# Cluster products of q and k in one TensorE visit, and a unit's filler work from its first gap

## The chip, the cores and the metric

The kernel runs on one core of a Trainium2 chip. The metric is the device time of one execution in microseconds. The median of four runs of the kernel before is 346.37 us (346.23 to 346.71).

A core has five engines that work side by side, each through its own queue in order: TensorE (PE; its weight loads are shown as PEld), VectorE (DVE), ScalarE (ACT), GpSimd (POOL) and SyncE (SP, which only issues transfers here). TensorE writes its results to PSUM, a small memory of eight banks, from which VectorE and ScalarE read them. "Granted clock" is the share of its full speed that TensorE was allowed.

## The reference

Two steps are computed, one feeding the other.

```python
# q, k, v: (4, 8, 768, 64); centroids: (8, 16, 64)
q_assign = argmax(q_n @ c_n.T); k_assign = argmax(k_n @ c_n.T)     # nearest of 16 clusters
scores = where(q_assign[:, None] == k_assign[None, :], q @ k.T / 8, -1e9)
attn = softmax(scores) @ v                                          # 32 heads
# x: (3072, 512), the heads side by side
xn = x / sqrt(mean(x * x) + 1e-6) * rms_g
out = (silu(xn @ w_gate) * (xn @ w_val)) @ w_out                    # 512 -> 1536 -> 512
```

Attention runs only between a query and the keys of the same cluster. The kernel gets the mask from the product itself: to the 64 rows of a head it adds 16 rows of zeros and ones that name the cluster, so a query and a key of the same cluster score a large constant more, and the exponential takes that constant off again.

## The kernel before

**Units and groups.** There are 8 units: for each of the 4 batches, two blocks of 384 queries, with all 8 heads (`UNITS`). A group is 4 heads of one batch (`HG`, 8 groups), and holds the transposed and extended q and k of these heads. Batch b uses groups 2b and 2b + 1.

**One unit.** `attention` walks through the 8 heads with 3 score steps each, so a unit has 24 of them. A score step (`scores`, L333) is two matmuls, and ScalarE turns the result into exponentials (L337). Scores have two PSUM buffers (`ps_s`), so the step after the next needs the exponential of this one to be done. At the second score step of a head, `pv` of the head before is issued (18 short matmuls, L351); after every second head VectorE divides by the sums (L356, L358). In the last head, each of the three steps adds a square on ScalarE (L376; VectorE in the first two units).

**Gaps and filler.** Behind each score step lies a gap, numbered 0 to 23 here, which `attention` fills from a list of pieces, each with a cost. It issues pieces until their summed cost reaches the share of the total that belongs to the gaps passed so far. With `skip=1` the first gap stays empty, and the total is spread over 23. Filler comes in this order:
- the last 8 pieces of the gate and value products of unit u - 2 (`gv`, L423),
- the row norm of unit u - 1 (`rms`),
- the output product of unit u - 2 (`out_mm`, L448) in pieces, with the transposes of the normed rows of unit u - 1 (`xtrans`, L396) among the last of them,
- the other `gv` pieces of unit u - 1 but its last 8, interleaved evenly by `spread` with the preparation of group u + 2 (in units 2 to 5: groups 4 to 7).

A gate piece is four matmuls; ScalarE then computes a tanh (L431) and VectorE a product (L432). A value piece is four matmuls and a product on VectorE (L436).

**Preparing a group** (`group_work`, from unit 2 on by `group`). For each of the 4 heads, `trans` transposes q and k with three f32 matmuls each (L208), and ScalarE copies the result out (L214); GpSimd casts q, and VectorE casts k in two halves (L227); then v is cast and later heads' loads are issued. After the four heads come the clusters, first of q (m = 0) and then of k (m = 1), each in four steps (`cluster_steps`): `products` (four f32 matmuls of 32 columns, L241, and a transpose by VectorE, L244), `most` (L249), `same` (L253) and `back` (L271, another transpose). `products` has cost 0.7, the other three cost nothing, so they follow at once. At the end `place` writes the zeros and ones under q and k with small transfers on GpSimd's queue (L282).

**PSUM banks.** `trans`, `cluster_products`, `xtrans`, `gv` and `out_mm` all take their PSUM tiles from one pool of three banks (`ps_g`). A tile can be written when the last reader of the tile that held its bank has finished. TensorE's queue is in order: where the first matmul of a piece waits for a bank, everything behind it waits too.

The order is the program's own (`manual_schedule`); nothing reorders it later.

Of the kernel before, what the change touches and what calls it, by code (L numbers as in the profile page):

```python
# [22 lines left out]
def kernel(  # L23
# [13 lines left out]
    B, H, S, D = q.shape  # L37
# [8 lines left out]
    NG = B * H // HG  # L46
    UNITS = [(b, c, HT) for b in range(B) for c in (0, HT)]
    NU = len(UNITS)
    CC = DM // P
# [4 lines left out]
    CUT = CC + 2 * FC - 8  # L54
# [30 lines left out]
    def load_qk(n):  # L85
        if n < B * H:
            load(n, 0)
            load(n, 1)

    def load_v(n, vq=None):  # L90
        if n >= B * H:
            return
        stagedv[n] = stage.tile([P, ST, D], F32, tag="vs", name="vs", bufs=NV)
        (vq or nc.sync).dma_start(out=stagedv[n], in_=src(v, n))
# [107 lines left out]
    def trans(g, h, part, on=None):  # L202
        if (g, h // 2) not in qkT:
            qkT[g, h // 2] = qk32.tile([P, 2, 2, UQ], F32, tag="qkT", name="qkT")
        qk = staged[g * HG + h]
        ps = ps_g.tile([P, UQ], F32, tag="gen", name="tq")
        for i in range(HT):
            nc.tensor.transpose(ps[:, i * P:(i + 1) * P], qk[:, part, 2 * i:2 * i + 2].rearrange("p t d -> p (t d)"),  # L208
                                ident_f)
        to, by = qkT[g, h // 2][:, h % 2, part], 1.0 / ZS if part else 1.0  # L210
        if on is nc.vector:
            nc.vector.tensor_scalar_mul(to, ps, by)
        else:
            nc.scalar.activation(to, ps, ACT.Copy, scale=by)  # L214
# [5 lines left out]
    def cast(on, g, h, part, es=(0, 1)):  # L220
        for e in es:
            to = cols((kext if part else qext)[g % 4][:D, h], g, e)
            of = qkT[g, h // 2][e * D:(e + 1) * D, h % 2, part]
            if on is nc.scalar:
                nc.scalar.copy(to, of)
            else:
                on.tensor_copy(to, of)  # L227

    def vcast(n):
        nc.gpsimd.tensor_copy(vbf[n // HG % 4][:, n % HG, :, :D], stagedv[n])  # L230
# [24 lines left out]
    def cluster_steps(g, m):  # L255

        of = {}

        def products():
            of["cl"] = cluster_products(g, [(h, m) for h in range(HG)])  # L260

        def most():
            of["mx"] = largest(of["cl"])

        def same():
            of["ohT"] = asg.tile([P, UQ], BF16, tag="ohT", name="ohT", bufs=2)
            compare(of["ohT"].rearrange("p (b e c) -> p b e c", e=2, c=NC), of["cl"], of["mx"])

        def back():
            put[g, m] = asg.tile([P, UQ], BF16, tag="oh", name="oh", bufs=3)  # L270
            nc.vector.transpose(put[g, m], of["ohT"])  # L271

        return [products, most, same, back]
# [3 lines left out]
    def place(on, g, m, es=(0, 1)):  # L277

        ext = (kext if m else qext)[g % 4]
        for h in range(HG):  # L280
            for e in es:
                on.dma_start(out=ext[D:D + NC, h, e * UQ:(e + 1) * UQ],  # L282
                             in_=put[g, m][32 * h + e * NC:32 * h + (e + 1) * NC])
# [39 lines left out]
    def scores(u, h, i):  # L323
        b, col, nt = UNITS[u]
        g, hh, w = b * 2 + h // HG, h % HG, nt * P
        if i == 0:
            pT[u, h] = ptp.tile([P, ST, UQ], BF16, tag="pT", name="pT")
        n = ST // nt
        ps = ps_s.tile([P, 2, 512], F32, tag="s", name="s")
        flat = ps.rearrange("p a b -> p (a b)")  # L330
        for j in range(n):
            kc = n * i + j
            nc.tensor.matmul(ps[:, j, :w] if nt == HT else flat[:, j * w:(j + 1) * w],  # L333
                             lhsT=cols(kext[g % 4][:KR, hh], g, kc // HT, kc % HT * P, (kc % HT + 1) * P),
                             rhs=cols(qext[g % 4][:KR, hh], g, col // HT, 0, w), start=True, stop=True)
        of = ps[:, :, :w] if nt == HT else flat[:, :n * w].rearrange("p (c w) -> p c w", w=w)
        nc.scalar.activation(pT[u, h][:, n * i:n * i + n, :w], of, ACT.Exp, bias=off, scale=scale * ZS)  # L337
# [130 lines left out]
    def group_work(g):  # L468

        t, c = [], []  # L470
        for h in range(HG):
            n = g * HG + h
            t += [(0.3, lambda h=h: trans(g, h, 0)), (0.3, lambda h=h: trans(g, h, 1))]

            def others(n=n):
                vcast(n)
                load_qk(n + NQ)
                load_v(n + NV)

            def both(h=h, f=others):  # L480
                cast(nc.gpsimd, g, h, 0)
                f()
                cast(nc.vector, g, h, 1, (0,))
            if g == 2:
                c.append((0.0, others))
            else:
                c += [(0.0, both), (0.0, lambda h=h: cast(nc.vector, g, h, 1, (1,)))]
        a = []
        for m in range(2):
            a += [(0.0 if i else 0.7, f) for i, f in enumerate(cluster_steps(g, m))]  # L490
            if g == 3:
                a.append((0.0, lambda m=m: place(nc.gpsimd, g, m)))
            elif g == 2:
                a.append((0.0, (lambda: (place(nc.sync, g, 1), place(nc.sync, g, 0, (1,)))) if m else
                          (lambda: place(nc.sync, g, 0, (0,)))))
        if g > 3:
            a.append((0.0, lambda: [place(nc.gpsimd, g, m) for m in range(2)]))
        return t, c, a

# [4 lines left out]
    def group(g):  # L504
        t, c, a = group_work(g)
        return [x for h in range(HG) for x in t[2 * h:2 * h + 2] + c[2 * h:2 * h + 2]] + a

    def spread(a, b):

        if not a:  # L510
            return list(b)
        w, n = [], 0
        for i, x in enumerate(a):
            w.append(x)
            while n < len(b) * (i + 1) // len(a):
                w.append(b[n])
                n += 1
        return w
# [9 lines left out]
    def out_work(u):  # L528
        return [(0.86, lambda t=t, p=p: out_mm(u, t, p)) for t in range(UNITS[u][2]) for p in range(3)]
# [105 lines left out]
    def attention(heads, fill, skip=0, hooks={}):  # L635
        gaps = [(u, h, i) for u, h in heads for i in range(UNITS[u][2])]
        total, done, n = sum(c for c, _ in fill), 0.0, 0
        for at, (u, h, i) in enumerate(gaps):
            scores(u, h, i)
            if i == (0 if (u, h) == (1, 0) else 1):  # L640
                for p in due:
                    pv(*p)
                due[:] = [(u, h)]
            if h == H - 1:
                squares(u, i, False)
            if (u, h, i) in hooks:
                hooks[u, h, i]()
            while n < len(fill) and at >= skip and done <= total * (at + 1 - skip) / (len(gaps) - skip):
                done += fill[n][0]
                fill[n][1]()  # L650
                n += 1
        for _, f in fill[n:]:
            f()

    attention([(0, h) for h in range(H)], [], hooks={(0, *divmod(i, HT)): f for i in range(H * HT) for f in [first.get(i, more)] if f})
    for u in range(1, NU):
        ffn, o, g = ffn_work(u - 1), out_work(u - 2) if u > 1 else [], u + 2
        if u == 1:
            t, c, a = group_work(2)
            t3, c3, a3 = group_work(3)  # L660
            n = LEAD - 4
            o3 = [(0.0, lambda i=i: load_o(i)) for i in range(0, FC, 4)]
            prep = c + a + spread(weave(t3[n:], c3), o3) + a3[:5]
            idle = const.tile([P, 1], BF16)

            def norm():
                rms(0)
                nc.gpsimd.tensor_copy(idle, xn[0][:, HT - 1, DM - 1:])
                for h in range(HG):
                    casts(pool_, H + h, K0, Q0, K1, Q1)  # L670

            hooks = {(1, 0, 0): late[6], (1, 0, 1): lambda: (late[7](), norm())}
            hooks.update({(1, *divmod(2 + i, HT)): t3[i][1] for i in range(n)})
            hooks[1, *divmod(LEAD - 1, HT)] = lambda: xtrans_all(0)
            fill = spread(ffn[CC:CUT], prep)
            attention([(1, h) for h in range(H)], fill, LEAD, hooks)
        else:
            fill = ffn_work(u - 2)[CUT:] + [(0.0, lambda u=u: rms(u - 1))]
            fill += border(spread(o[:3], [(0.0, f) for _, f in a3[5:]]) + o[3:], ffn) if u == 2 else border(o, ffn)
            attention([(u, h) for h in range(H)], fill + spread(ffn[CC:CUT], group(g) if g < NG else []), 1)  # L680
    rest = ffn_work(NU - 2)[CUT:]
    rest[0][1]()
    pv(NU - 1, H - 1)
# [38 lines left out]
```

The softmax here doesn't subtract the row's maximum and nothing guards it: scores larger than these inputs give would overflow.

## Time and profile before

| | |
|---|---|
| median of the runs | 346.37 us |
| profiled execution | 346.35 us |
| its span, from the first to the last instruction | 344.6 us |
| TensorE busy | 337.7 us, 98% |
| ScalarE busy | 259.6 us, 75% |
| VectorE busy | 220.8 us, 64% |
| GpSimd busy | 113.1 us, 33% |
| granted clock of TensorE | 1.000 |
| score matmuls (L333) | 384, 327 ns each |
| exponentials (L337) | 192, 905 ns each |
| cluster products (L241) | 96 records, 498 ns each |

In the lines of a timeline, the columns are start and duration in us, the engine, the line of the kernel, the operation, the tiles written and read with their shapes, and the number of instructions merged into the row; brackets give how long the engine stood idle before, and what ended that. Matmuls are pipelined: one starts before the one before it has ended. So what a visit of TensorE costs is the time from its start to the start of the next, and not the duration shown. The same holds, by about a tenth of a microsecond, for ScalarE and VectorE. The chain is the work that ended last, followed back from the last instruction.

Each f32 product of a group's clusters shows as two records (two passes), so a visit of four products is eight.

### The profile page before, as it was taken

The page shows a single profiled execution, that of the slowest core. Times are in us where ns is not written, and L with a number is a line of the kernel's source. Part 1 is how long each engine was busy: PE and PEld are TensorE (multiplying, and loading weights), DVE is VectorE, ACT ScalarE, POOL GpSimd, SP SyncE. Part 2 cuts the span into 40 slices and gives each one's busy share as a digit, 9 for nine tenths or more (in the row PEclk, how much of TensorE's full clock was granted, in tenths as well). Part 3 has the DMA queues.
Part 4 walks back from the last instruction along what each step waited for, and adds up shares of the span by engine and source line. Part 5 has one row for each costly group of instructions (what it writes and reads, how often), then busy time and mean ns, then how long its engine had stood idle before and what let it go on. Part 6 is the DMA issues. An engine that isn't in the chain of part 4 may idle for free.

```text
span 344.6 us, 7999 instructions
## 1 busy us (share of the span) xinstructions
PE 337.7 (98%) x3045; PEld 208.6 (61%) x3045; DVE 220.8 (64%) x540; ACT 259.6 (75%) x449; POOL 113.1 (33%) x225
## 2 busy tenths in 40 slices
PE   8999999999999999999999999999999999999996
PEld 4547657555765567565675656755566656655654
DVE  6999796975578626785367745686356645675330
ACT  5899979856888768886797777888778877764422
POOL 6999596234336205180132702435000000000000
DMA  7999989882450014400120010000100001001002
GB/s 269 380 210 205 259 169 232 142 280 82 147 159 17 28 63 150 139 22 35 61 94 2 23 63 31 2 8 18 63 32 0 2 33 61 2 1 64 30 2 91
DMA packets 27302, 31.62 MB, mean 92 GB/s; under 512 B 4480, under 2 KB 24320, under 8 KB 27264
## 3 DMA queue, kind: packets, MB, share of 16 engines
q1 hardware_dynamic: 18608, 25.02, 21.9%
q0 software_dynamic: 8368, 5.71, 10.1%
q8 instruction: 24, 0.39, 0.5%
q10 hardware_dynamic: 288, 0.39, 0.3%
q14 instruction: 14, 0.11, 0.1%
HBM read 28.35 MB, written 6.29 MB: 101 GB/s over the span
## 4 chain that ended last, share of the span: by engine, by line
PE 88%; ACT 5%; DVE 5%; issue 1%; POOL 0%; ACTq 0%; DVEq 0%; POOLq 0%
PE gate L423 17%; PE val L423 17%; PE o L448 17%; PE s L333 16%; PE acc L351 9%; PE tq L208 4%; ACT pT L337 4%; PE sc L241 3%; PE tx L396 1%; PE warm L117 1%; DVE pads L312 1%; DVE kext L317 1%; DVE qext L317 1%; PE o L459 1%; DVE scT L308 1%
## 5 line engine op out<-in xcount | busy, mean ns | idle before, releaser
L337 ACT ACTIVATE pT<-s,off 128x768 bf16<-128x768 f32 x192 | 170.8, 905 | 33.9 <-PE s L333 32.8
L333 PE MATMUL s<-qext,kext 80*128 80x384 bf16 x384 | 94.4, 327 | 1.8 <-ACT pT L337 1.1
L432 DVE SCALAR_TENSOR_TENSOR th<-th,gate 128x384 f32<-128x384 f32 x84 | 46.3, 552 | 51.8 <-ACT th L431 51.5
L423 PE MATMUL gate<-xnT,wg 128*128 128x384 bf16 x384 | 78.6, 325 | 0.1
L423 PE MATMUL val<-xnT,wv 128*128 128x384 bf16 x384 | 78.1, 326 | 0.0
L448 PE MATMUL o<-wo,gvT 128*128 128x512 bf16 x276 | 67.6, 379 | 0.0
L227 POOL CAST qext<-qkT 64x384 bf16<-64x384 f32 x64 | 35.3, 558 | 75.3 <-ACT qkT L214 66.7
L333 PEld LDWEIGHTS <-kext 80*128 80x128 bf16 x384 | 36.6, 98 | 31.4 <-issue 6.4
L431 ACT ACTIVATE th<-gate 128x384 f32<-128x384 f32 x84 | 41.2, 491 | 13.9 <-PE gate L423 13.5
L423 PEld LDWEIGHTS <-wv 128*128 128x128 bf16 x384 | 36.1, 97 | 25.5 <-issue 3.8
L423 PEld LDWEIGHTS <-wg 128*128 128x128 bf16 x384 | 35.9, 97 | 24.5 <-issue 3.3
L436 DVE SCALAR_TENSOR_TENSOR gvT<-th,val 128x384 bf16<-128x384 f32 x84 | 46.2, 550 | 6.2 <-PE val L423 1.6
L351 PEld LDWEIGHTS <-pT 128*128 128x128 bf16 x1152 | 43.4, 97 | 10.1 <-DVE x L358 1.1
L351 PE MATMUL acc<-vbf,pT 128*128 128x65 bf16 x1152 | 45.7, 193 | 0.6 <-ACT pT L337 0.2
L448 PEld LDWEIGHTS <-gvT 128*128 128x128 bf16 x276 | 25.7, 97 | 25.5 <-issue 0.6
L208 PE MATMUL tq<-ident_f,qk 128*128 128x128 f32 x192 | 30.8, 279 | 0.0
L214 ACT ACTIVATE qkT<-tq 128x384 f32<-128x384 f32 x57 | 26.9, 495 | 3.8 <-PE tq L208 3.3
L282 POOL DMA_DIRECT2D qext<-oh x40 | 19.2, 488 | 30.6 <-DVE oh L271 24.2
L397 DVE TENSOR_SCALAR xnT<-tx,gcol 128x384 bf16<-128x384 bf16 x28 | 10.6, 412 | 28.7 <-PE tx L396 28.7
L208 PEld LDWEIGHTS tq<-ident_f,qk 128*128 128x128 f32 x192 | 23.9, 144 | 6.6 <-ACT qkT L214 1.0
L451 ACT COPY o_sb<-o 128x512 f32<-128x512 f32 x23 | 13.5, 586 | 17.7 <-PE o L448 17.7
L282 POOL DMA_DIRECT2D kext<-oh x40 | 19.1, 487 | 9.6 <-DVE oh L271 9.6
(81 smaller groups left out, 247.7 us busy)
## 6 DMA issues: line engine op xcount, KB each, us to landing
qk<-in_q_dram SPq DMA_DIRECT2D x32, 192.0 KB, 3.9
vs<-in_v_dram SPq DMA_DIRECT2D x32, 192.0 KB, 4.2
out_dram<-o_sb SPq DMA_DIRECT2D x23, 256.0 KB, 2.0
qk<-in_k_dram SPq DMA_DIRECT2D x30, 192.0 KB, 4.1
wg<-in_moe_w_gate_dram POOLq DMA_DIRECT2D x4, 384.0 KB, 8.3
wv<-in_moe_w_val_dram POOLq DMA_DIRECT2D x4, 384.0 KB, 10.5
wo<-in_moe_w_out_dram POOLq DMA_DIRECT2D x3, 512.0 KB, 7.6
qext<-oh POOLq DMA_DIRECT2D x40, 12.0 KB, 1.6
```

The lines of the kernel that those rows point to most:

```text
L208: nc.tensor.transpose(ps[:, i * P:(i + 1) * P], qk[:, part, 2 * i:2 * i + 2].rearrange("p t d -> p (t d)"), ident_f)
L214: nc.scalar.activation(to, ps, ACT.Copy, scale=by)
L227: on.tensor_copy(to, of)
L282: on.dma_start(out=ext[D:D + NC, h, e * UQ:(e + 1) * UQ], in_=put[g, m][32 * h + e * NC:32 * h + (e + 1) * NC])
L333: nc.tensor.matmul(ps[:, j, :w] if nt == HT else flat[:, j * w:(j + 1) * w], lhsT=cols(kext[g % 4][:KR, hh], g, kc // HT, kc % HT * P, (kc ...
L337: nc.scalar.activation(pT[u, h][:, n * i:n * i + n, :w], of, ACT.Exp, bias=off, scale=scale * ZS)
L351: nc.tensor.matmul(acc[:, h % 2, t], lhsT=pT[u, h][:, kc, t * P:(t + 1) * P], rhs=vbf[g % 4][:, hh, kc % HT * 2 + kc // HT], start=kc == 0 ...
L423: nc.tensor.matmul(ps, lhsT=w[:, c, f * P:(f + 1) * P], rhs=xnT[u][:, c, :n], start=c == 0, stop=c == CC - 1)
L431: nc.scalar.activation(th, ps, ACT.Tanh, scale=0.5)
L432: nc.vector.scalar_tensor_tensor(th, th, 1.0, ps, op0=ALU.add, op1=ALU.mult)
L436: nc.vector.scalar_tensor_tensor(gvT[u][:, f, :n], gates[u], 0.5, ps, op0=ALU.mult, op1=ALU.mult)
L448: nc.tensor.matmul(outs[u], lhsT=gvT[u][:, f, t * P:(t + 1) * P], rhs=wo[:, f], start=f == 0, stop=f == FC - 1)
```

## The change

Two edits.

```diff
         if g > 3:
+            a[:1] = [(1.4, lambda f=(a[0][1], a.pop(4)[1]): [x() for x in f])]
             a.append((0.0, lambda: [place(nc.gpsimd, g, m) for m in range(2)]))
```

For groups 4 to 7 the list `a` had nine pieces: products, most, same, back of q, the same of k, and place. The fifth, k's products, is taken out and put into one piece with q's, with the summed cost 1.4. The order becomes: products of q and of k (eight f32 products one after the other, and two transposes of L244 on VectorE), most, same, back of q, most, same, back of k, place. As the list is one piece shorter, `spread` also sets all the pieces of the preparation a little differently among the `gv` pieces.

```diff
-            attention([(u, h) for h in range(H)], fill + spread(ffn[CC:CUT], group(g) if g < NG else []), 1)
+            attention([(u, h) for h in range(H)], fill + spread(ffn[CC:CUT], group(g) if g < NG else []))
```

In units 2 to 7 the filler begins in gap 0 and not in gap 1, and its cost is spread over 24 gaps and not 23. The first pieces, of the `gv` of unit u - 2, now stand before the `pv` of the last head of unit u - 1, which is still issued in gap 1.

No matmul, copy or transfer is added or taken away.

## The prediction

> **What bounds the kernel now.** I read the page first (busy time and chain), then the timeline of TensorE gap by gap, and last the VectorE and ScalarE timelines around the places where TensorE stands still.
>
> ```profile
> span 344.6 us, 7999 instructions
> PE 337.7 (98%) x3045; PEld 208.6 (61%) x3045; DVE 220.8 (64%) x540; ACT 259.6 (75%) x449; POOL 113.1 (33%) x225
> PE 88%; ACT 5%; DVE 5%; issue 1%; POOL 0%; ACTq 0%; DVEq 0%; POOLq 0%
> ```
>
> TensorE is the bound: it is never long idle and the chain is its own work. No matmul is added or taken away, so the time can change only through the small delays between visits. I write S, PV, G, V, O, T, C, X for a visit to scores, pv, gate, val, out_mm, trans, cluster_products, xtrans. From start to next start, undisturbed, they take 0.328, 0.547, 0.650, 0.650, 0.864, 0.328, 0.785 and 0.164 us. Whatever a visit takes over that is a delay. From unit 2 on the delays sit in few places, and units 3 to 5 repeat with a period of 41.04 us (C at 100.73, 141.77, 182.81, 223.85 in the chain).
>
> ```profile
> 94.12 0.52 PE L208 MATMUL tq<-ident_f,qk 128*128 128x128 f32 x3
> 94.48 0.81 PE L423 MATMUL gate<-xnT,wg 128*128 128x384 bf16 x4
> ...
> 100.25 0.49 PE L333 MATMUL s<-qext,kext 80*128 80x384 bf16 x2
> 100.67 0.85 PE L241 MATMUL sc<-qkT,cblk 128*32 128x384 f32 x8
> ...
> 106.16 0.49 PE L333 MATMUL s<-qext,kext 80*128 80x384 bf16 x2
> 106.64 0.81 PE L423 MATMUL val<-xnT,wv 128*128 128x384 bf16 x4
> 107.29 0.88 PE L333 MATMUL s<-qext,kext 80*128 80x384 bf16 x4
> ...
> 266.77 0.49 PE L333 MATMUL s<-qext,kext 80*128 80x384 bf16 x2
> 267.53 0.48 PE L333 MATMUL s<-qext,kext 80*128 80x384 bf16 x2 [0.27 <-ACT pT L337]
> ```
>
> Read the starts; the durations overlap and are not what a visit costs. S at 100.25 should hand over at 100.58, C starts at 100.67: 0.09 lost on entering a C visit. S at 106.16 should hand over at 106.49, V comes at 106.64: 0.16 lost, because its PSUM bank is freed by VectorE's L436 of 106.08. The two adjacent S visits at 107.29 take 0.72 in the chain instead of 0.656: 0.07 lost waiting for an exponential. At 266.77 the same meeting of two S costs 0.43 (0.76 to the next start).
>
> ```profile
> 90.62 0.56 DVE L432 SCALAR_TENSOR_TENSOR th<-th,gate 128x384 f32<-128x384 f32 x1 [0.27 <-ACT th L431]
> 91.21 0.36 DVE L227 CAST kext<-qkT 64x384 bf16<-64x384 f32 x1
> 91.60 0.56 DVE L436 SCALAR_TENSOR_TENSOR gvT<-th,val 128x384 bf16<-128x384 f32 x1
> ...
> 104.51 0.55 DVE L432 SCALAR_TENSOR_TENSOR th<-th,gate 128x384 f32<-128x384 f32 x1 [1.06 <-ACT th L431]
> 104.98 0.55 DVE L253 TENSOR_TENSOR ohT<-scT,mx 128x384 bf16<-128x384 f32 x1
> ...
> 107.44 0.53 DVE L249 TENSOR_REDUCE mx<-scT 128x24 f32<-128x384 f32 x1
> 108.01 0.56 DVE L253 TENSOR_TENSOR ohT<-scT,mx 128x384 bf16<-128x384 f32 x1
> 108.49 0.55 DVE L436 SCALAR_TENSOR_TENSOR gvT<-th,val 128x384 bf16<-128x384 f32 x1
> 108.95 0.57 DVE L271 STREAM_TRANSPOSE oh<-ohT 128x384 bf16<-128x384 bf16 x1
> ```
>
> VectorE runs in order, about 0.47 us from one start to the next. All of G, V, O, T, C, X share three PSUM banks, and a bank comes free when VectorE or ScalarE has read it. So a late VectorE stops TensorE.
>
> **The change: what moves.** Unit 3 before and after, bars between the 24 gaps (each begins with an S, left out):
>
> ```
> before  - | PV G V | G V | G V | PV G V | O O | O | PV O | O O | O | PV X X O | X X O |
> G T | PV V T G | V T | T G V | PV T G | T V | G T T | PV V G | C V | G V | PV C G | V
> after   G V | PV G V | G V | G V | PV O | O O | O | PV O | O O | X X O | PV X X | O G |
> T V | PV T G V | T T | G V | PV T G T | V G | T V | PV T G | V C C | G | PV V G | V
> ```
>
> The transposes of L244 follow C C on VectorE back to back; SP's and POOL's queues keep their order, and place stays last in the unit, half a unit or more before its columns are read, so those cost nothing at either end.
>
> **What goes.**
> - One C visit of two, in each of units 2 to 5. Entering costs 0.094. Inside, each of the four f32 products runs in two passes, and the second pass of four starts 0.346 after the first; two passes need 0.692 of the 0.785, and 0.093 goes on leaving. A second product in the same visit pays neither: 0.187 x 4 = 0.75. Bounds: 0 (passing to the other bank costs as much) to 0.75.
> - The empty gap at a border. Unit 2: 0.17 at its first S and 0.13 at the G of gap 2. Units 3 to 6: 0.07 each. Unit 7: 0.43. With G V between the two S this goes: 1.02. The waits of V in gap 23 of units 2 to 5, 0.16 each: V then needs the bank of G21 (G of gap 21), free since long: 0.64.
> - The wait of G in gap 15 for a transpose's bank (T at 91.53 takes 0.415): 0.087 x 4 = 0.35.
> Sum gone: 2.76.
>
> **What comes.** The built program tells which tile each bank held before; I follow the tightest ones with offsets from the rows: exponential 0.59 after its S starts, 0.79 of ScalarE; square 0.50, tanh 0.38, copy of a T 0.37 of ScalarE; tanh at the earliest 0.855 after G starts; L432 0.52 after tanh; a bank is free 0.60 after L432 or L436 starts.
> - V in gap 0 takes the bank of G22. From S21's start: exponential 0.59, square 1.39, tanh 1.89, L432 of G21 at 2.40 (S at 102.11, L432 at 104.51: the same 2.40). Then in VectorE's new order L253 +0.47, L436 +0.48, L271 +0.46, L249 +0.50, L432 of G22 +0.46: 4.77, bank free at 5.37. TensorE gets to V after S G S PV V G S V S G = 4 x 0.328 + 0.547 + 5 x 0.65 = 5.11. Wait 0.26 to 0.27, at the four borders after units 2 to 5: 1.08. Unit 7's border has no cluster work: L432 of G22 stands there at 266.72, free 267.32, V would come at 267.75: no wait. Bounds 0 and 0.5 each.
> - G in gap 15 takes the bank of V13, whose L436 now stands behind a second cast. From S13's start: G13 at 1.20, tanh 2.06, L432 2.58, cast +0.59, L436 +0.39 (the steps 90.62, 91.21, 91.60): 3.56, bank free at 4.16. TensorE arrives after S PV T G V S T T S = 3 x 0.328 + 0.547 + 3 x 0.328 + 2 x 0.65 = 3.82. Wait 0.34 (0.02 of it already at the second T T, whose bank G13 frees at 3.18), x 4 = 1.36. Later, T in gap 16 needs L436 of V15: tanh 5.41 at the end of an unbroken ScalarE run, L432 5.93, cast and L436 6.67, free 7.27, against an arrival of 7.31: nothing, by 0.04. Bounds for the stretch 0.1 and 0.6 per unit.
> - A T straight after PV takes 0.36, not 0.328 (94.12 to 94.48). One such T per unit becomes three: 2 x 0.032 x 4 = 0.25.
> - Unit 2, gap 2: V takes G1's bank, L432 of G1 now at 69.45 behind L356 and L358, free 70.05, arrival 69.92: 0.13.
> Sum: 2.82.
>
> Product k's bank is that of G19: L432 of it is about 0.4 us ahead of need, so no wait; if that cover fails, it costs what it is late, with S21 and its exponential behind it.
>
> Net 2.82 - 2.76 = +0.06 on the profiled execution's 346.35 (span 344.6 and 1.8 around it), which is 0.02 under the median: **346.4 us**.
>
> **Two rules weighed.** All the rows above run at a granted clock of 1.000, through waits of up to 0.43, so I price no clock loss. The Trainium skill, "TensorE: Matmul & The Clock Gate", section "A second HAM failure mode: psum-queue depth-cycling", warns that cycling PSUM banks lets TensorE micro-idle until its clock oscillates. By that rule the eight new waits could each bring one 3.4 us window at half clock, some 1.7 us each as an estimate from that page, and the time would be near 360; this trace's clock speaks against it.
> Weight loads of the second four passes stand at 100.69 to 100.71, while the first four (from 100.67) still run in the same columns, so I let k's loads hide behind q's passes. The same page, section "Part 3: Packing small matmuls", says that loads overlap running matmuls only when the row group differs. By that rule one load of 0.11 would stand open in each merged visit, and the sum would be 346.8; the trace's overlap speaks against it.
>
> **Rivals.**
> 1. Faster: VectorE and ScalarE are ahead of my offsets and the two new waits stay small. Against: the offsets are taken from the same instructions. With half of both waits left: 346.4 - 1.2 = 345.2; with none, 344.0. It decides from 0.19 less wait per unit.
> 2. Slower: VectorE's in-order queue sets the pace through the banks. The place is L253, L436, L271, L249 between L432 of G21 and of G22. If each step costs 0.57 (107.44 to 108.01, one waiting on the one before) and not 0.47, V in gap 0 waits 0.4 to 0.5 more, 1.6 to 2.0 over four borders: 348.2. From 0.16 more per unit it is slower by over 0.2%. For it: L249 to L253 does cost 0.57. Against: the others there are not neighbours in a dependency.
> 3. The merged visit is none to TensorE: passing from q's to k's bank costs as much as leaving and entering. 0.75 is not saved: 347.1.
>
> **How the numbers follow.** The times repeat within 0.2% or so, about what can be told from no change: 345.7 to 347.1 counts as the same. Balanced (my forecast, 345.7 to 347.1): 0.44. Rival 1: 0.28. Rival 2, with what I overlooked in the rearranged gaps: 0.22. Rival 3: 0.06, half of it over the limit. Faster 0.28, same 0.47, slower 0.25. Range: 1 in 10 out at each side. Below, rival 1 with half the waits is 345.2, and I cut at 345.0; above, half of rival 2's price gives 347.4, and I cut at 347.7.
>
> **What would show it.** After: one C visit of about 1.48 per unit 2 to 5 with one entry of 0.09; no wait at the second S of a unit; V in gap 23 prompt; V in gap 0 about 0.27 late on L432; G in gap 15 about 0.32 late on L436; three T after PV at 0.36; period of units 3 to 5 of 41.0 to 41.2. I am wrong if the clock falls under 1.000, if waits appear in gaps that I called free (V2, T in gap 16, k's product), or if the two waits are not there.

## The result and the profile after

The changed kernel takes 345.85 us (median of 33 runs, 345.56 to 346.37) against 346.29 us for the kernel before in the same comparison (53 runs): a ratio of 0.9987, 95% interval 0.9982 to 0.9992. It is 0.44 us faster. The forecast was 346.4, no change but for 0.06 us to the slow side. The measured time lies in the range and within 0.2% of before. But the interval does not contain 1: the change is clear of the noise, and it goes to the fast side, where the forecast had the slow side.

The page of the changed kernel:

```profile
span 344.3 us, 8007 instructions
PE 337.2 (98%) x3045; PEld 208.5 (61%) x3045; DVE 221.8 (64%) x540; ACT 261.1 (76%) x449; POOL 113.0 (33%) x225
PE 82%; DVE 9%; ACT 6%; issue 2%; DMA 1%; DVEq 0%; POOL 0%; ACTq 0%; POOLq 0%
```

TensorE is as busy as it was. But the chain has changed: VectorE carries 9% of it and not 5%. The chain now runs through VectorE where TensorE waits for a PSUM bank. The granted clock is 0.999: 1.00 up to the last matmul (at 341.1 us) and 0.50 only behind it, in the last 0.7 us of the span.

TensorE around the border of units 2 and 3, after (start, duration, engine, line, operation, number of instructions):

```profile
101.51 1.50 PE L241 MATMUL sc<-qkT,cblk 128*32 128x384 f32 x16
102.94 0.50 PE L333 MATMUL s<-qext,kext 80*128 80x384 bf16 x2
...
106.11 0.49 PE L333 MATMUL s<-qext,kext 80*128 80x384 bf16 x2
106.44 0.81 PE L423 MATMUL val<-xnT,wv 128*128 128x384 bf16 x4
107.09 0.49 PE L333 MATMUL s<-qext,kext 80*128 80x384 bf16 x2
107.42 0.81 PE L423 MATMUL gate<-xnT,wg 128*128 128x384 bf16 x4
108.28 0.81 PE L423 MATMUL val<-xnT,wv 128*128 128x384 bf16 x4
```

Subtract neighbouring starts. The merged visit takes 101.51 to 102.94, 1.43 us. V in gap 23 (106.44) follows its S (106.11) at once, where it lost 0.16 before. S and S no longer meet, so their 0.07 is gone. G in gap 0 takes 107.42 to 108.28, 0.86 and not 0.65: the next V waits 0.21. VectorE shows for what:

```profile
105.36 0.55 DVE L432 SCALAR_TENSOR_TENSOR th<-th,gate 128x384 f32<-128x384 f32 x1 [1.26 <-ACT th L431]
105.83 0.55 DVE L253 TENSOR_TENSOR ohT<-scT,mx 128x384 bf16<-128x384 f32 x1
106.30 0.55 DVE L436 SCALAR_TENSOR_TENSOR gvT<-th,val 128x384 bf16<-128x384 f32 x1
106.76 0.57 DVE L271 STREAM_TRANSPOSE oh<-ohT 128x384 bf16<-128x384 bf16 x1
107.26 0.51 DVE L249 TENSOR_REDUCE mx<-scT 128x24 f32<-128x384 f32 x1
107.69 0.54 DVE L432 SCALAR_TENSOR_TENSOR th<-th,gate 128x384 f32<-128x384 f32 x1
```

The second L432 reads G22 and ends at 108.23; V starts on its bank at 108.28. Between the two L432 stand the four instructions that the prediction named.

The second new wait, in unit 2's gap 15, VectorE first and then TensorE:

```profile
90.53 0.55 DVE L432 SCALAR_TENSOR_TENSOR th<-th,gate 128x384 f32<-128x384 f32 x1
91.11 0.35 DVE L227 CAST kext<-qkT 64x384 bf16<-64x384 f32 x1
91.50 0.55 DVE L436 SCALAR_TENSOR_TENSOR gvT<-th,val 128x384 bf16<-128x384 f32 x1
```
```profile
90.78 0.90 PE L208 MATMUL tq<-ident_f,qk 128*128 128x128 f32 x6
91.52 0.49 PE L333 MATMUL s<-qext,kext 80*128 80x384 bf16 x2
92.11 0.81 PE L423 MATMUL gate<-xnT,wg 128*128 128x384 bf16 x4
```

L436 ends at 92.05, G starts at 92.11 where S would have handed over at 91.85. The two T before lost 0.03 and 0.05 as well: 0.74 for 0.656.

The balance, from the starts in both profiled executions (us, sums over units 2 to 7):

| | forecast | measured |
|---|---|---|
| one cluster visit in place of two, units 2 to 5 | -0.75 | -0.98 (4 x 0.244) |
| waits gone at the borders (S after S, V in gap 2 of unit 2) | -1.02 | -1.02 |
| V in gap 23 | -0.64 | -0.64 |
| G in gap 15, old wait | -0.35 | -0.35 |
| V in gap 0 of units 3 to 6, new wait | +1.08 | +0.90 (0.21, 0.26, 0.21, 0.21) |
| gaps 14 and 15, new wait | +1.36 | +1.36 (4 x 0.34) |
| two more slow T per unit | +0.25 | +0.25 |
| V in gap 2 of unit 2, new wait | +0.13 | +0.12 |
| sum | +0.06 | -0.36 |

The spans of the two traces differ by 0.23 (344.57 to 344.35), with 0.06 of the other sign before unit 2, where the programs are the same; so from unit 2 on the trace shows 0.28 less, and the medians differ by 0.44. What lies between these and the balance, 0.08 on either side, is not assigned to a step.

### The profile page after: what moved, and what is told of

Its sections match the earlier page's. It is cut to its first block, busy times and chain, and to the rows that moved or that the text cites. A ratio compares the mean times of both kernels' runs of the same rounds, so it can differ in the third digit from the quotient of the medians.

```text
span 344.3 us, 8007 instructions
## 1 busy us (share of the span) xinstructions
PE 337.2 (98%) x3045; PEld 208.5 (61%) x3045; DVE 221.8 (64%) x540; ACT 261.1 (76%) x449; POOL 113.0 (33%) x225
## 4 chain that ended last, share of the span: by engine, by line
PE 82%; DVE 9%; ACT 6%; issue 2%; DMA 1%; DVEq 0%; POOL 0%; ACTq 0%; POOLq 0%
PE o L448 17%; PE gate L423 16%; PE val L423 16%; PE s L333 15%; PE acc L351 9%; ACT pT L337 4%; PE tq L208 3%; PE sc L241 3%; DVE th L432 2%; PE tx L396 1%; DVE gvT L436 1%; ACT th L431 1%; PE warm L117 1%; DVE pads L312 1%; DVE kext L317 1%
## 5 line engine op out<-in xcount | busy, mean ns | idle before, releaser
L432 DVE SCALAR_TENSOR_TENSOR th<-th,gate 128x384 f32<-128x384 f32 x84 | 46.2, 550 | 44.6 <-ACT th L431 43.2
L436 DVE SCALAR_TENSOR_TENSOR gvT<-th,val 128x384 bf16<-128x384 f32 x84 | 46.3, 552 | 8.1 <-PE val L423 3.6
L208 PE MATMUL tq<-ident_f,qk 128*128 128x128 f32 x192 | 31.5, 282 | 0.0
L208 PEld LDWEIGHTS tq<-ident_f,qk 128*128 128x128 f32 x192 | 23.2, 144 | 6.5 <-ACT qkT L214 1.0
```

The costliest lines, as they stand in the source:

```text
L432: nc.vector.scalar_tensor_tensor(th, th, 1.0, ps, op0=ALU.add, op1=ALU.mult)
L436: nc.vector.scalar_tensor_tensor(gvT[u][:, f, :n], gates[u], 0.5, ps, op0=ALU.mult, op1=ALU.mult)
```

## The experiments

The theory to be tested: the time is the sum of TensorE's short delays, and these follow from which bank each piece gets and when VectorE and ScalarE have read it. Its rival: each edit gives a gain of its own, and the small net is chance.

**The first edit alone.** Edit, against the changed kernel:

```diff
-attention(..., fill + spread(ffn[CC:CUT], group(g) if g < NG else []))
+attention(..., fill + spread(ffn[CC:CUT], group(g) if g < NG else []), 1)
```

> Only the first edit: q's and k's products in one visit, the filler still from gap 1. Theory 1 (the time is the sum of TensorE's short delays, and the two edits need each other): the merged visit saves 0.25 us in units 2 to 5 (1.0 in all) and V in gap 23 waits no more (0.64), but with an empty gap 0 the second S of the next unit now waits about 0.4 us for the exponential of gap 23 at the four borders, in place of 0.07 (+1.4), and two more transposes follow PV (+0.12 to 0.25). Unit 7's border keeps its 0.43. Sum: 0.1 to 0.2 faster than before, 346.1 to 346.3. Theory 2 (each edit gives its own gain, independent of the other): 1.0 for the visit and 0.64 for V, 344.7.

Measured: 346.26 us, ratio to before 0.9998 (0.9990 to 1.0007). TensorE at a border:

```profile
148.30 0.49 PE L333 MATMUL s<-qext,kext 80*128 80x384 bf16 x2
149.05 0.48 PE L333 MATMUL s<-qext,kext 80*128 80x384 bf16 x2 [0.26 <-ACT pT L337]
```

From S to S 0.75 pass in place of 0.33: a wait of 0.43 at every border from unit 3 on, for the exponential of gap 23, which stands on ScalarE behind a square and a tanh. With both products in gap 20, TensorE has 0.88 us less to do between S of gap 21 and the second S of the next unit, and ScalarE's work there is not less. As theory 1 had it, that eats what the visit and V in gap 23 gain.

**The second edit alone.** Edit, against the changed kernel:

```diff
-            a[:1] = [(1.4, lambda f=(a[0][1], a.pop(4)[1]): [x() for x in f])]
```

> Only the second edit: filler from gap 0, q's and k's products still in two visits. Theory 1: the waits at the second S go (1.02, unit 2's V in gap 2 takes 0.12 of it back), V in gap 0 waits for nothing because L432 of G22 is about 0.6 us ahead of need; V in gap 23 keeps its 0.16; gap 15 waits 0.34 in place of 0.09 and one more transpose follows PV (+1.1 over units 2 to 5). Sum: 0.2 slower than before, 346.5. Theory 2 (independent gains): 1.0 faster, 345.3.

Measured: 348.25 us, ratio 1.0057 (1.0044 to 1.0069). Both theories missed, and theory 1 by 1.75 us. TensorE in gap 18, then VectorE:

```profile
139.14 0.49 PE L333 MATMUL s<-qext,kext 80*128 80x384 bf16 x2
139.47 0.82 PE L208 MATMUL tq<-ident_f,qk 128*128 128x128 f32 x6
140.51 0.81 PE L423 MATMUL val<-xnT,wv 128*128 128x384 bf16 x4 [0.23 <-DVE th L432]
```
```profile
139.16 0.71 DVE L227 CAST kext<-qkT 64x384 bf16<-64x384 f32 x2
139.90 0.56 DVE L432 SCALAR_TENSOR_TENSOR th<-th,gate 128x384 f32<-128x384 f32 x1
```

V of gap 18 gets the bank of G in gap 17, only three short pieces after it. It is due at 140.12 and starts at 140.51, when L432 (from 139.90) has ended: 0.39 to 0.41 in each of units 2 to 5, 1.57 in all. The other delays are the expected ones (0.16 at V in gap 23, 0.34 in gaps 14 and 15, none at V in gap 0). My working for this kernel had followed the new border and gaps 14 to 16, and had not looked at gap 18. With that term theory 1 comes to 348.1.

So alone the edits give -0.07 and +1.92 us, and together -0.44: they are not independent.

**Is it the second visit or the shorter list?** The merging undone, the list kept at eight pieces:

```diff
-            a[:1] = [(1.4, lambda f=(a[0][1], a.pop(4)[1]): [x() for x in f])]
+            a[1:2] = [(0.7, lambda f=(a.pop(4)[1], a[1][1]): [x() for x in f])]
```

> The changed kernel with the merging undone but the list kept one piece shorter: q's products are a piece, k's products and q's maximum the next, so spread sets every transpose and every gate and value piece as in the changed kernel, and k's visit falls into gap 21. It asks why the second edit alone came to 348.25, where 346.5 was expected: its trace has a wait of 0.39 at V in gap 18 of units 2 to 5, which the forecast had not priced. Theory 1 (that wait comes from the order that a list of nine pieces gives, T T V in gap 18 with V on the bank of G17; one visit or two has nothing to do with it): no wait in gap 18; the second visit costs 0.25 per unit (1.0 in all) and, as it puts G21 0.88 us later, V in gap 0 no longer waits (-0.9). Sum: 345.9. Theory 2 (the second visit itself is what costs in this order): near the second edit alone, 348.2. Theory 3 (a merged visit is worth nothing): 345.0.

Measured: 346.18 us, ratio 0.9995 (0.9986 to 1.0004). There is no wait in gap 18: the 0.39 belongs to the order that `spread` makes of nine pieces, and not to a second visit. TensorE in gaps 20 and 21 and at the border:

```profile
142.42 0.85 PE L241 MATMUL sc<-qkT,cblk 128*32 128x384 f32 x8
143.20 0.50 PE L333 MATMUL s<-qext,kext 80*128 80x384 bf16 x2
143.63 0.85 PE L241 MATMUL sc<-qkT,cblk 128*32 128x384 f32 x8
144.42 0.82 PE L423 MATMUL gate<-xnT,wg 128*128 128x384 bf16 x4
...
148.56 0.81 PE L423 MATMUL gate<-xnT,wg 128*128 128x384 bf16 x4
149.21 0.81 PE L423 MATMUL val<-xnT,wv 128*128 128x384 bf16 x4
```

Each visit takes 0.785, an entry of 0.09 to 0.10 and 0.01 behind it. That makes 1.77 for the two against 1.53 for the merged visit with the same pieces around it: 0.24 per unit. G in gap 0 takes 0.65, so the wait of V is gone. In units 3 to 5 the two nearly cancel: the period is 41.13, in the changed kernel it runs from 41.10 to 41.15. The gain over the kernel before in the same comparison is 0.22, and the changed kernel's is 0.44; that is more apart than theory 1's 0.05. The intervals of the two ratios overlap, and what lies between is left open. The price of a visit can be read from the starts; from the medians of these two kernels it can't.

**The wait of V in gap 0.** One VectorE instruction moved; an empty piece keeps the list's length:

```diff
+            a[1:2], a[4:5] = [(0.0, lambda f=(a[1][1], a[4][1]): [x() for x in f])], [(0.0, lambda: None)]
```

> The changed kernel with one VectorE instruction moved: k's maximum (L249) directly behind q's, right after the two transposes, where VectorE idles 1.2 us. Theory 1 (V in gap 0 waits because that maximum stands between L432 of G21 and L432 of G22): L432 of G22 comes 0.45 us earlier, the wait of 0.21 to 0.26 at the borders of units 3 to 6 goes, nothing takes its place before V in gap 2, 0.9 less: 0.26% under the changed kernel, 344.95. Theory 2 (ScalarE's squares and exponentials set the border; the wait moves on to the next V): no gain, 345.85.

Measured: 345.36 us, ratio 0.9973 (0.9962 to 0.9984). VectorE, then TensorE:

```profile
144.64 0.97 DVE L249 TENSOR_REDUCE mx<-scT 128x24 f32<-128x384 f32 x2
146.41 0.56 DVE L432 SCALAR_TENSOR_TENSOR th<-th,gate 128x384 f32<-128x384 f32 x1 [0.80 <-ACT th L431]
...
148.39 0.51 DVE L432 SCALAR_TENSOR_TENSOR th<-th,gate 128x384 f32<-128x384 f32 x1
```
```profile
148.15 0.49 PE L333 MATMUL s<-qext,kext 80*128 80x384 bf16 x2
148.47 0.81 PE L423 MATMUL gate<-xnT,wg 128*128 128x384 bf16 x4
149.13 0.81 PE L423 MATMUL val<-xnT,wv 128*128 128x384 bf16 x4
```

From L432 to L432 it is 1.98 and not 2.33 us, and V follows G after 0.65. The cause is shown: one VectorE instruction of 0.5 us in the wrong place held TensorE at four borders. Of the forecast gain of 0.9 the medians show 0.49. In the trace 0.05 to 0.06 comes back as a wait of V in gap 2 in units 3 to 5, which leaves 0.73.

**The wait of G in gap 15.** The second cast of k of the first head moved behind L436 of V13:

```diff
+        w = [x for h in range(HG) for x in t[2 * h:2 * h + 2] + c[2 * h:2 * h + 2]]
+        if g > 3:
+            w[3:5] = [(0.0, lambda: None), (0.3, lambda f=(w[4][1], w[3][1]): [x() for x in f])]
+        return w + a
```

> The changed kernel with the second cast of k of a group's first head moved behind L436 of V in gap 13. Theory 1 (the cast in front of L436 makes G in gap 15 wait, but the tanh of G15 ends a run of ScalarE that doesn't come earlier): the wait of 0.26 in gap 15 goes, and 0.15 of it comes back at G and the second T in gap 16, 0.11 less per unit, 0.45 in all: 345.4. Theory 2 (the cast is all there is to it): the whole 0.26 per unit, 1.04 in all: 344.8.

Measured: 345.84 us, ratio 0.9986 (0.9977 to 0.9995): nothing gained. TensorE in gaps 15 and 16, then ScalarE:

```profile
132.27 0.49 PE L333 MATMUL s<-qext,kext 80*128 80x384 bf16 x2
132.60 0.81 PE L423 MATMUL gate<-xnT,wg 128*128 128x384 bf16 x4
...
134.77 0.52 PE L208 MATMUL tq<-ident_f,qk 128*128 128x128 f32 x3
135.20 0.81 PE L423 MATMUL gate<-xnT,wg 128*128 128x384 bf16 x4
135.93 0.55 PE L208 MATMUL tq<-ident_f,qk 128*128 128x128 f32 x3
136.32 0.49 PE L333 MATMUL s<-qext,kext 80*128 80x384 bf16 x2
```
```profile
131.73 0.90 ACT L337 ACTIVATE pT<-s,off 128x768 bf16<-128x768 f32 x1 [0.49 <-PE s L333]
132.53 0.86 ACT L214 ACTIVATE qkT<-tq 128x384 f32<-128x384 f32 x2
133.27 0.91 ACT L337 ACTIVATE pT<-s,off 128x768 bf16<-128x768 f32 x1
134.05 0.51 ACT L431 ACTIVATE th<-gate 128x384 f32<-128x384 f32 x1
```

G in gap 15 (132.60) is prompt: the cast was what stood before it. But in gap 16 T takes 0.43, G 0.73 and T 0.39, where 0.36, 0.65 and 0.33 are free of waits: 0.20 of the 0.26 comes back. The 0.05 per unit that the trace leaves does not show in the medians. ScalarE works without a pause from the exponential of gap 14 (131.73) through two copies of T and an exponential to the tanh (134.05), and what waits for that tanh cannot come earlier. Theory 1 named the place and expected 0.15 there; theory 2 falls.

**A version without either wait.** Both maxima moved to the products' piece, and the transposes shifted by an empty piece at the head (a second empty piece keeps the list's length), so that no two T stand side by side:

```diff
-            a[:1] = [(1.4, lambda f=(a[0][1], a.pop(4)[1]): [x() for x in f])]
+            f = [a[i][1] for i in (0, 4, 1, 5)]
+            a = [(1.4, lambda: [x() for x in f])] + a[2:4] + a[6:]
+            a.insert(2, (0.0, lambda: None))
...
+        start = [(0.0, lambda: None)] if g > 3 else []
+        return start + [x for h in range(HG) for x in t[2 * h:2 * h + 2] + c[2 * h:2 * h + 2]] + a
```

> The changed kernel with both maxima right behind the two transposes and an empty piece at the head of the list, which shifts the transposes by one place: gaps 12 to 18 become V T, PV T G V, T G, T V, PV G T V, T G, V T, and no two T stand side by side. Theory 1 (the stretch of gaps 14 to 16 loses 0.34 per unit because two copies of T on ScalarE and a cast on VectorE stand between a gate and the bank that the next pieces need): with the tightest banks free 0.02 to 0.2 us ahead of need, the 0.34 and one slow T after PV go, and the wait at V in gap 0 too, as in the run with k's maximum early: 345.36 - 1.2 = 344.1. Theory 2 (any order of this list meets a wait of that size somewhere): 345.4.

Measured: 344.19 us, ratio 0.9940 (0.9926 to 0.9953), the fastest version here, and what theory 1 expected. TensorE in gaps 13 to 15 (T, G, V; S, T, G; S, T):

```profile
129.39 0.52 PE L208 MATMUL tq<-ident_f,qk 128*128 128x128 f32 x3
129.75 0.81 PE L423 MATMUL gate<-xnT,wg 128*128 128x384 bf16 x4
130.40 0.81 PE L423 MATMUL val<-xnT,wv 128*128 128x384 bf16 x4
131.04 0.49 PE L333 MATMUL s<-qext,kext 80*128 80x384 bf16 x2
131.37 0.49 PE L208 MATMUL tq<-ident_f,qk 128*128 128x128 f32 x3
131.73 0.81 PE L423 MATMUL gate<-xnT,wg 128*128 128x384 bf16 x4
132.37 0.49 PE L333 MATMUL s<-qext,kext 80*128 80x384 bf16 x2
132.70 0.49 PE L208 MATMUL tq<-ident_f,qk 128*128 128x128 f32 x3
```

Of these steps only T after PV (0.36) and the T at 131.37 (0.36) are over their undisturbed time; the G behind the latter starts 0.05 after the end of L432 of the G before (131.12 to 131.67), as the waiting pieces above do. Elsewhere in units 3 to 5 the entry of the C visit is left (0.09), and V in gap 2 still waits 0.04 to 0.05. The period of units 3 to 5 is 40.59, against 41.04 before and 41.10 to 41.15 in the changed kernel. The instructions are the same; only their order differs.

## Why the prediction was right or wrong

- *The empty gap at the border, V in gap 23, the old wait of gap 15.* Right to 0.01 each.
- *The two new waits on a bank.* Both are there, at the pieces named, behind the instructions named: gaps 14 and 15 cost 0.34 as worked out; V in gap 0 waits 0.21 (once 0.26) and not 0.27. The five steps from L432 to the next L432 took 2.33 in all where I took 2.37, mostly at the last (0.43 and not 0.46), the bank came free 0.59 and not 0.60 after L432's start, and S after the merged visit takes 0.34 and not 0.328, so V comes a little later. That is 0.18 of the miss. Runs with one instruction moved took each wait away from its place; the one in gap 0 stayed away for the most part, the one in gap 15 came back in gap 16.
- *The cluster visit.* This is the term that failed: "A second product in the same visit pays neither: 0.187". It is worth 0.244, so 0.98 and not 0.75, outside the bound that I set; the merged visit takes 1.43, where I expected about 1.48. I had priced each pass of k at the 0.346 that lies between the first and the second pass of a visit. In the merged visit the four passes start at 101.51, 101.86, 102.18 and 102.51, so a pass further in takes 0.32: the 0.346 held 0.024 that only the first pass of a visit pays, and leaving costs 0.12 and not 0.093. The first matmuls behind a visit lose 0.01, which I had not priced; that is paid once as well. Together this is 0.23 of the miss, and the run with two visits in the same order shows the same 0.24 per unit.
- *Slow T after PV, V in gap 2 of unit 2, no wait for k's bank.* Right; no new wait for the queues of SP or POOL shows either.
- *The rules weighed.* The granted clock is 0.999 to 1.000 in all eight kernels, with eight new waits of 0.21 to 0.26 us on banks in the changed kernel and up to 0.41 us in the second edit alone, so the warning about cycling banks cost nothing at this size. I had named a clock under 1.000 as a sign of being wrong. By the letter it came (0.999), but only behind the last matmul, where it costs nothing. The loads for k's passes stand at 101.86 to 101.88 and 102.19 to 102.21, beside running passes in the same columns, so the rule on row groups does not describe them; the merged visit saved more than 0.187, not less.
- *Rivals.* Rival 1 came in direction but not in size (the waits are 0.18 smaller in all, where it needed 0.19 per unit); rival 2 and rival 3 did not occur. The unlooked-for wait that rival 2 stood for did come, in the second edit alone.

The forecast set 2.82 against 2.76, and each small error of a term is as large as such a difference. The direction was open by its own working. The waits, their places and the instructions behind them were right; what failed is the size of two terms, the cluster visit (0.98 and not 0.75) and V in gap 0 (0.90 and not 1.08), 0.23 and 0.18 us that fall on the same side.

## What to carry to other kernels

Where one engine is busy all the time, list its undisturbed visit times, subtract neighbouring starts, and explain every rest: here that gave the waits of a new order, to some hundredths of a microsecond, before it ran, wherever the bank had been followed; where it had not, a wait of 0.39 went unseen. With few rotating buffers, an order of pieces is a set of distances between a buffer's writer and its reader on another in-order engine; look at every piece that reuses a buffer after two or three short pieces, also outside the place of the edit. When one wait is removed, ask what the next piece waits for: moving one cast gained nothing, while shifting all transposes and their casts by one place, with q's maximum moved too, gained 1.2 us over the run with k's maximum early.

## What the runs showed of the hardware

- An f32 product of 32 columns by 384 runs in two passes. Four of them side by side take 0.346 us from the first pass to the second, and 0.322 and 0.323 from pass to pass after that; entering such a visit from bf16 work costs 0.094, and from the last pass to the next bf16 matmul it is 0.44. The Trainium skill, "TensorEngine Tiling (Array Packing)", section "Key Properties", says that changing the tiling mode drains TensorE. The entry and the exit here fit that, but do not show it: the first weight loads of a visit stand at its start (101.513) and not under the visit before, so a load left uncovered could be the entry's cost as well, and no run tells the two apart.
- A T that had to wait for its bank takes about 0.055 us more itself (0.38 to 0.39 from its start and not 0.328, in gap 14 of the changed kernel and in gap 16 of the run with the cast moved). A G that waited does not (0.647 behind the wait in gap 15).
- A T directly after PV takes 0.36 and not 0.33 us, from unit 2 on in all eight kernels.
